# New per-engine orders, statistics by per-partition scalars and fewer warm-up matmuls in a retention and SoLU kernel

## Chip, cores and metric

The kernel runs on one core of a Trainium2 chip. The metric is device time in microseconds (us), the median over runs.

## What is computed

A retention step over q, k and v (8 batches, 8 heads, 576 positions, head size 64), whose output becomes 4,608 tokens of width 512, followed by a feed-forward block with a SoLU activation and a layer norm:

```python
scores = scale * np.matmul(q, k.transpose(0, 1, 3, 2))
gamma = 1.0 - 2.0 ** (-5.0 - np.arange(H, dtype=np.float32))
Dmat = np.where(rel >= 0, gamma[:, None, None] ** rel[None, :, :], 0.0)
attn_out = np.matmul(scores * Dmat[None, :, :, :], v)
x = np.ascontiguousarray(attn_out.transpose(0, 2, 1, 3)).reshape(B * S, H * D)
h = x @ w_in                                  # 512 -> 1024
h_max = np.max(h, axis=-1, keepdims=True)
e = np.exp(h - h_max)
solu = h * (e / (np.sum(e, axis=-1, keepdims=True) + 1e-09))
mu = np.mean(solu, axis=-1, keepdims=True)
var = np.mean((solu - mu) ** 2, axis=-1, keepdims=True)
out = ((solu - mu) / np.sqrt(var + 1e-06) * g_ln) @ w_out   # 1024 -> 512
```

Retention is computed in chunks: inside a chunk by scores and a mask, between chunks by a state k-transposed times v that is carried on with a decay.

## The kernel before

**Tiles.** The sequence of a batch is cut into two windows of 256 positions and a rest of 64; the rests of four batches form one window together. That makes 18 windows. A window is worked in two halves of four heads each, so there are 36 half-windows i. Each window also yields two blocks of 128 tokens, so there are 36 token tiles t for the feed-forward part.

**Steps of a half-window i.** `ldq`, `ldk`, `ldv` load 256 KB each (SP queue). `sq`, `sk` scale q and k to 16 bit and `cv` casts v (GpSimd, called POOL; for i = 0 and 1 sq is on VectorE, called DVE, and cv on ScalarE, called ACT). `T` transposes q and k on TensorE (PE), `qe` takes them out of PSUM (ACT). `S` computes scores, `mask` multiplies them by the mask (DVE). `K` computes k-transposed times v into PSUM. `sa` and `sd` add it to the carried state (DVE), `sm` multiplies by the decay (POOL, L441) and `sc` casts the state to 16 bit in two instructions (POOL, L450). `I` multiplies q by that state, `V` the masked scores by v, into the same PSUM tile, which `xe` takes out as xT (ACT). The last windows of a group of four batches (i = 16, 17, 34, 35) have no K and no state steps. K of the next half-window comes after V of this one, so K, sa, sd, sm, sc, I, V form a loop through three engines.

**Steps of a token tile t.** `M1` is the product with w_in, eight matmuls (L468). `em` negates it out of PSUM and finds the row minimum (DVE, L479), `ex` the exponential with its row sum se (ACT, L491), `so` the product of the two with its row sum su (DVE, L501; this is VectorE's product), `va` the row sum sv of the squared deviations (ACT, L510). `L` transposes the product and `le` takes it out (ACT). `M2` is the product with w_out (L560). For the first NE = 14 tiles the mean is removed after M2 by `od` (DVE); for later ones the weights are centred beforehand (`wp`, DVE). `x` (per window, L519 and L522, on DVE) makes the variance from se and sv, `rs` its power of -0.5 (POOL, L530), `oe` scales the output tile (ACT) and `out` stores it (SP).

**Order.** Every engine works its instructions strictly in program order. The table FIRST (L29 to L102) holds one written list of step names for each engine and for the SP queue. `order_ops` (L113) replays these lists with the durations in DUR and buffer limits in CAP, only to interleave the emission; it never changes the order in a list. So what each engine does next is what FIRST says, and a step that isn't ready holds all that stands behind it on its engine. A load in SP's list stands behind stores that may still wait for their `oe`.

**Start.** Twelve matmuls on zeros run first (L747). Then, up to time WARM = 31 of the replayed schedule and ahead of the first M2, the gaps that the replay sees on PE are filled with further matmuls on zeros (L755), 33 in all.

Of the kernel before, what the change touches and what calls it, by code (L numbers as in the profile page):

```python
# [11 lines left out]
P = 128  # L12
# [6 lines left out]
    sq=1.03, sk=1.03, st_b=0.4, cast=0.84, rs=0.6, cv=0.61,  # L19
    ld=0.89, ldw=1.34, out=0.72, lm=0.42,  # L20
# [4 lines left out]
WARM = 31.0  # L25
NE = 14
WPOOL = ()

FIRST = dict(  # L29
    ACT=(  # L30
        "cv1 cv0 qe0 xe0 qe1 qe2 wi1a wi3a wi2a xe1 wi0a ex0 xe2 qe3 qe4 ex1 le0 xe3 qe5 wg6 va1 "
        "le1 wg2 wg0 wg4 xe4 ex2 nw va0 qe6 xe5 ex3 le2 oe0 va2 ex4 qe7 oe1 va3 qe8 xe6 qe9 xe7 "
        "oe2 le3 va4 ex5 oe3 le4 va5 qe10 xe8 ex6 xe9 le5 oe4 qe12 ex7 ex8 le6 oe5 qe11 xe10 va6 "
        "va7 le7 xe11 ex9 oe6 qe13 va8 va9 oe7 le8 xe12 ex10 qe14 ex11 xe13 le9 va10 oe8 qe15 "
        "ex12 xe14 le10 oe9 va11 qe16 va12 xe15 le11 oe10 ex13 qe17 ex14 qe18 oe11 xe16 va13 le13 "
        "va14 le12 xe17 ex15 qe19 oe13 le14 va15 qe20 ex17 xe18 oe12 qe21 ex16 xe19 oe14 qe22 "
        "va17 le15 va16 ex18 oe15 le16 le17 xe20 oe16 xe21 ex19 va18 qe23 va19 oe17 ex20 le18 "
        "xe22 qe24 ex21 xe23 oe18 le19 va21 le20 va20 oe19 qe25 xe24 ex23 qe26 oe20 xe25 ex22 "
        "le21 va23 qe27 va22 le23 oe21 le22 ex24 qe28 xe26 ex25 xe27 oe22 qe29 va24 va25 ex26 "
        "le24 oe23 qe30 xe28 le25 oe24 qe31 ex27 xe29 oe25 va26 qe32 va27 le26 ex28 le27 xe30 "  # L40
        "ex29 xe31 oe26 qe33 va28 va29 oe27 ex30 le28 ex31 xe32 qe34 xe33 oe28 qe35 va31 le29 "
        "va30 xe34 ex32 le30 xe35 ex33 oe29 va32 va33 ex35 oe30 le31 va35 le32 ex34 oe31 le35 "
        "va34 le34 oe32 oe35 le33 oe34 oe33"
    ),
    DVE=(
        "sq1 sq0 sa0 sd0 mask0 sa1 sd1 mask1 wi1b wi2b sa2 gc sd2 wi3b wi0b mask2 em0 sa3 sd3 so0 "
        "em1 mask3 wg7 so1 sa4 sd4 mask4 em2 wg1 wg5 wg3 mask5 sa5 em3 sd5 so2 x0 wp3 wp0 sa6 od0 "
        "sd6 mask6 em4 so3 od1 em5 sa7 sd7 mask7 so4 x1 od2 sa8 mask8 sd8 em6 od3 so5 sa9 mask9 "
# [12 lines left out]
        "T0 K0 S0 I0 V0 T1 K1 S1 T2 I1 S2 V1 K2 G M1_0 I2 V2 T3 K3 M1_1 T4 S3 L0 I3 V3 S4 K4 T5 "
        "M1_2 L1 I4 V4 K5 S5 M1_3 WM M2_0 T6 I5 V5 K6 S6 L2 M1_4 M2_1 T7 M1_5 I6 T8 V6 K7 S7 M2_2 "
        "T9 I7 V7 S8 K8 L3 M1_6 M2_3 I8 V8 K9 S9 L4 M1_7 T10 M2_4 I9 V9 K10 S10 L5 M1_8 T12 M2_5 "
        "L6 M1_9 T11 I10 V10 K11 S11 M2_6 L7 I11 V11 K12 S12 T13 M1_10 M2_7 I12 L8 V12 S13 K13 "
        "M1_11 T14 M2_8 I13 V13 K14 S14 L9 M1_12 T15 M2_9 L10 I14 V14 S15 K15 M1_13 T16 M2_10 I15 "
        "V15 S16 L11 M1_14 T17 M2_11 T18 I16 S17 V16 M1_15 L13 I17 V17 K18 S18 L12 M2_13 T19 "
        "M1_17 L14 I18 S19 V18 K19 T20 M2_12 M1_16 T21 M2_14 I19 V19 S20 K20 T22 M1_18 L15 I20 "
        "V20 S21 K21 M2_15 L16 M1_19 L17 M2_16 I21 V21 K22 S22 T23 M1_20 M2_17 I22 S23 V22 K23 "
        "L18 M1_21 T24 M2_18 I23 V23 S24 K24 L19 M1_23 L20 M2_19 T25 I24 M1_22 V24 K25 S25 T26 "
        "M2_20 I25 V25 S26 K26 L21 M1_24 T27 M2_21 L23 I26 V26 K27 S27 L22 M1_25 T28 M2_22 I27 "  # L70
        "V27 K28 S28 T29 M1_26 M2_23 L24 M1_27 T30 I28 V28 S29 K29 L25 M2_24 T31 I29 V29 K30 S30 "
        "M2_25 M1_28 T32 I30 V30 S31 K31 L26 M1_29 L27 M2_26 I31 V31 K32 S32 T33 M1_30 M2_27 "
        "M1_31 L28 I32 V32 S33 K33 T34 M2_28 I33 V33 S34 T35 M1_32 L29 I34 S35 V34 L30 M1_33 I35 "
        "V35 M2_29 M1_35 L31 M2_30 M1_34 L32 M2_31 L35 M2_32 L34 M2_35 L33 M2_34 M2_33"
    ),
    POOL=(
        "sk0 sm0 sc0 sk1 sk2 sq2 sm1 sc1 cv2 sm2 sc2 sq3 sk3 cv3 sk4 sq4 sm3 sq5 sc3 cv4 sk5 cv5 "
        "sm4 sc4 sk6 sq6 cv6 sm5 sc5 sk7 sk8 rs0 sq8 sq7 sm6 cv8 sc6 cv7 sq9 sk9 sm7 sc7 cv9 rs1 "
        "cv11 sk10 sm8 sc8 sq12 sq10 cv13 cv10 sm9 sc9 sk12 rs2 sq11 sm10 sc10 sk11 cv12 sq13 "
        "sq16 sk13 sm11 sc11 sq14 sk14 rs3 sm12 sc12 cv14 sm13 sc13 sq15 cv16 sk15 sm14 rs4 cv17 "  # L80
        "sc14 sk16 cv15 cv18 sm15 sc15 sq17 rs5 sk17 sk18 sq18 sq19 sk19 sq21 cv19 rs6 sk21 sk20 "
        "sm18 cv21 sc18 sq20 sq22 sk22 sm19 sc19 cv20 rs7 sm20 sc20 cv22 sk23 rs8 sq23 cv25 sm21 "
        "sk24 sc21 sm22 sq24 cv23 sc22 cv24 sk25 sq25 sm23 rs9 cv26 sc23 sk26 sq26 sm24 sq27 sc24 "
        "rs10 sm25 sc25 sq29 sk27 sm26 cv28 cv29 sc26 cv27 sk28 cv30 sq28 sk29 rs11 sm27 sc27 "
        "sq30 sq31 sk30 sk31 sm28 sc28 rs12 sq32 cv32 sm29 sc29 sq34 sm30 sc30 sk32 cv35 cv31 "
        "sk33 sm31 sq33 sc31 rs13 cv33 sq35 sk34 sm32 sc32 sk35 cv34 sm33 sc33 rs14 rs15 rs16 "
# [3 lines left out]
        "ldk0 ldq1 ldv1 ldq0 ldv0 ldk1 lm ldv2 ldq2 ldk2 lwi3 lwi1 lwi2 lwi0 ldq3 ldk3 ldv3 ldk4 "  # L90
        "ldq4 ldq5 ldk5 ldv4 lwo6 ldv5 lwo0 lwo2 lwo4 ldk6 ldq6 ldv6 ldk7 ldv7 ldk8 ldq9 ldq8 "
        "ldq7 ldk9 ldv8 ldk10 ldq10 ldv9 out0 ldv11 ldv10 ldk12 ldq12 ldk11 ldv12 out1 ldv16 out2 "
        "ldv13 ldq16 ldq15 ldq13 ldk15 ldk14 out3 ldq11 ldk16 out4 ldk13 ldv17 ldv14 ldq14 ldk17 "
        "out6 ldq17 ldv15 ldq18 out5 ldq22 out7 ldv18 out8 ldk18 ldv21 ldv20 ldq19 ldk21 out9 "
        "ldk19 ldv19 ldk20 ldq21 ldq23 ldv22 ldv23 ldq20 ldk22 out11 out13 out10 ldk25 ldk24 "
        "ldv26 ldv25 ldq26 out12 ldk23 ldk29 ldv24 ldq25 ldv30 ldq24 ldk26 out14 out15 ldq27 "
        "out16 ldq31 ldk28 ldv27 ldv28 ldv29 out17 ldq28 ldv33 out18 ldk27 out19 ldq29 ldk31 "
        "ldq30 ldq32 ldv35 ldv31 ldk30 ldk33 out20 out22 ldq34 ldv32 ldk34 ldk32 out21 ldv34 "
        "ldq35 out23 ldk35 ldq33 out24 out26 out25 out27 out28 out29 out30 out31 out32 out35 "
        "out34 out33"  # L100
# [107 lines left out]
def kernel(  # L208
# [21 lines left out]
               xT=5, h=1, hn=3, e=2, oc=2, solu=3, sq=2, sml=8, lnT=4, o=1, osb=3)  # L230
# [52 lines left out]
    mhalf = small[:, 68:69]  # L283

# [156 lines left out]
    def state_cast(i):  # L443
        w, hf = divmod(i, 2)
        b, wi = wins[w]
        k = n_state[wi]
        n_state[wi] += 1
        s16 = sbd[wi][k % len(sbd[wi])]
        for e in range(2):
            nc.gpsimd.tensor_copy(out=s16[ee[e], :, :, ee[e]], in_=st[i]["g"][ee[e]])  # L450
        cur.setdefault((b, hf), {}).update({"g": st[i]["g"], wi: s16})
# [63 lines left out]
    def stats(w):  # L515
        d = ws[w]
        x = pools["sml"].tile([P, 2], FP, tag="w", name="w")
        d["x2"] = pools["sml"].tile([P, 2], FP, tag="w2", name="w2")
        nc.vector.scalar_tensor_tensor(  # L519
            out=x, in0=d["se"], scalar=1e-6, in1=d["se"], op0=ALU.mult, op1=ALU.mult  # L520
        )
        nc.vector.scalar_tensor_tensor(  # L522
            out=d["x2"], in0=d["sv"], scalar=float(DFF) ** -3, in1=x, op0=ALU.mult, op1=ALU.add
        )
# [263 lines left out]
```

## Time and profile before

| what | value |
|---|---|
| three runs | 246.45, 247.33, 356.75 us |
| median | 247.33 us |
| time of the profiled execution | 246.69 us |
| its span, first to last instruction | 244.9 us |
| busy: PE, DVE, ACT, POOL | 214.4, 182.9, 172.2, 172.7 us |
| mean granted TensorE clock | 0.992 |
| read from memory, written | 32.71 MB, 9.44 MB |

In the profile PE is the matmul engine and PEld its weight loads, which overlap it; a name with q at its end (SPq, POOLq) is an engine's sequencer. L468 is line 468 of the program. A row of the timeline gives start, length, engine, line, operation, output and input; in square brackets stands how long the engine sat idle before it and what released it. A window's row gives its length, then busy time (and instructions) of PE, PEld, DVE, ACT and POOL, the granted TensorE clock, the share of the DMA engines and GB/s; where only PE was asked for, its busy time alone stands ahead of the clock. Times lie on the span of one execution, 1.8 us shorter than that execution's device time.

### The profile page before, as it was taken

What the parts mean: (1) busy time and instruction counts of PE and PEld (TensorE: products, weight loads), DVE (VectorE), ACT (ScalarE), POOL (GpSimd) and SP (SyncE); (2) the same over time, 40 slices, a digit from 0 to 9 for tenths busy, and PEclk for the clock granted to TensorE, in tenths of its full rate; (3) what the DMA queues carried; (4) which work ended last, traced back from release to release, by engine and by line L of the source; (5) the groups of instructions that cost most, each with busy time, mean ns of one, the idle gap of its engine ahead of it and who ended that gap; (6) DMA issues with size and microseconds to landing.
All of it is one profiled execution on the core that took longest, in us unless ns stands there. A gap on an engine that the chain in (4) does not pass through costs nothing.

```text
span 244.9 us, 7426 instructions
## 1 busy us (share of the span) xinstructions
PE 214.4 (88%) x2998; PEld 124.1 (51%) x2998; DVE 182.9 (75%) x328; ACT 172.2 (70%) x301; POOL 172.7 (71%) x223
## 2 busy tenths in 40 slices
PE   8968887998997788999799889899869999999992
PEld 2435543554554445556456446455445554565550
DVE  7166899887995799989979767849845776897520
ACT  2234786767776597889769685868756687989971
POOL 2097994998959868799968969939995789631020
PEclk9999999999999999999999999999979999999999
DMA  7999999196886065798297865662516550510244
GB/s 188 322 367 300 352 295 269 30 246 170 226 236 185 3 170 175 193 305 237 63 256 196 264 175 136 170 172 82 178 29 188 156 150 4 129 46 23 65 94 120
DMA packets 65633, 42.62 MB, mean 174 GB/s; under 512 B 4024, under 2 KB 59456, under 8 KB 65600
## 3 DMA queue, kind: packets, MB, share of 16 engines
q1 hardware_dynamic: 65200, 41.96, 61.8%
q8 instruction: 23, 0.38, 0.6%
q10 hardware_dynamic: 400, 0.21, 0.4%
q14 instruction: 10, 0.08, 0.1%
HBM read 32.71 MB, written 9.44 MB: 172 GB/s over the span
## 4 chain that ended last, share of the span: by engine, by line
PE 33%; POOL 31%; DVE 13%; DMA 9%; issue 7%; ACT 5%; SPq 1%; POOLq 0%; DVEq 0%; ACTq 0%
POOL sbd L450 9%; PE h_ps L468 8%; POOL k L308 7%; PE o_ps L560 7%; POOL q L308 6%; PE xy L348 6%; POOL g L441 4%; DMA qr<-in_q_dram 4%; POOL v L316 3%; PE tln L536 3%; DVE ret L416 3%; DMA out_dram<-o_sb 2%; PE tqk L325 2%; DVE hn L479 2%; PE wm L755 2%
## 5 line engine op out<-in xcount | busy, mean ns | idle before, releaser
L468 PE MATMUL h_ps<-w_in,xT 128*128 128x512 f16 x288 | 68.8, 382 | 0.9 <-ACT w_in L612 0.9
L501 DVE SCALAR_TENSOR_TENSOR solu<-hn,e_sb 128x1024 f16<-128x1024 f32 x36 | 47.7, 1326 | 5.3 <-ACT e_sb L491 5.3
L479 DVE TENSOR_SCALAR_CACHE_REDUCE hn<-h_ps 128x1024 f32<-128x1024 f32 x36 | 43.8, 1218 | 9.9 <-PE h_ps L468 9.8
L491 ACT ACTIVATE e_sb<-hn,nm 128x1024 f32<-128x1024 f32 x36 | 41.4, 1151 | 8.0 <-DVE hn L479 6.2
L416 DVE TENSOR_TENSOR ret<-s_ps,masks 128x1024 f16<-128x1024 f32 x36 | 43.7, 1215 | 2.5 <-PE s_ps L383 2.5
L308 POOL TENSOR_TENSOR k<-kr,small 128x512 f16<-128x512 f32 x36 | 42.1, 1175 | 4.3 <-DMA kr<-in_k_dram 3.6
L510 ACT ACTIVATE sq<-solu,su 128x1024 f32<-128x1024 f16 x36 | 41.3, 1148 | 1.2 <-DVE solu L501 1.2
L308 POOL TENSOR_TENSOR q<-qr,small 128x512 f16<-128x512 f32 x34 | 39.4, 1165 | 3.7 <-DMA qr<-in_q_dram 3.0
L468 PEld LDWEIGHTS <-xT 128*128 128x128 f16 x288 | 27.0, 99 | 28.7 <-issue 2.0
L560 PEld LDWEIGHTS <-lnT 128*128 128x128 f16 x288 | 26.8, 98 | 28.7 <-issue 0.8
L441 POOL TENSOR_TENSOR g<-tt,small 128x128 f32<-128x128 f32 x32 | 17.1, 534 | 30.7 <-DVE tt L437 30.2
L560 PE MATMUL o_ps<-w2c,lnT 128*128 128x512 f16 x160 | 37.8, 379 | 0.1
L450 POOL CAST sbd<-g 64x256 f16<-64x256 f32 x64 | 34.8, 544 | 3.0
L456 ACT CAST xT<-xy 128x512 f16<-128x512 f32 x36 | 21.0, 584 | 21.3 <-PE xy L348 19.0
L333 ACT COPY qkT<-tqk 128x512 f32<-128x512 f32 x36 | 20.9, 579 | 15.4 <-PE tqk L325 15.3
L530 POOL TENSOR_TENSOR rs<-w,small 128x2 f32<-128x2 f32 x18 | 15.2, 846 | 20.3 <-DVE w L519 12.7
L348 PE MATMUL xy<-qkT,sbd 128*128 128x128 f16 (+1 forms) x128 | 13.5, 214 | 16.4 <-POOL sbd L450 15.8
L316 POOL CAST v<-vr 128x512 f16<-128x512 f32 x34 | 27.1, 801 | 0.8 <-PE xy L348 0.2
L560 PE MATMUL o_ps<-w2g,lnT 128*128 128x512 f16 x112 | 26.5, 379 | 0.6 <-DVE oc L568 0.6
L544 ACT COPY lnT<-tln 128x512 f32<-128x512 f32 x36 | 20.8, 577 | 5.7 <-PE tln L536 5.4
L536 PE MATMUL tln<-ident,solu 128*128 128x128 f16 x288 | 22.1, 220 | 0.5 <-ACT qkT L333 0.4
L536 PEld LDWEIGHTS <-solu 128*128 128x128 f16 x288 | 17.9, 98 | 6.5 <-issue 0.8
(53 smaller groups left out, 260.1 us busy)
## 6 DMA issues: line engine op xcount, KB each, us to landing
kr<-in_k_dram SPq DMA_DIRECT2D x32, 256.0 KB, 5.3
qr<-in_q_dram SPq DMA_DIRECT2D x32, 256.0 KB, 5.1
vr<-in_v_dram SPq DMA_DIRECT2D x32, 256.0 KB, 5.0
out_dram<-o_sb SPq DMA_DIRECT2D x64, 128.0 KB, 2.4
w_in_f<-in_moe_w_in_dram SPq DMA_DIRECT2D x4, 512.0 KB, 6.6
w_f<-in_moe_w_out_dram SPq DMA_DIRECT2D x4, 512.0 KB, 6.6
vr<-in_v_dram SPq DMA_DIRECT2D x16, 64.0 KB, 3.1
qr<-in_q_dram SPq DMA_DIRECT2D x16, 64.0 KB, 2.0
```

Source lines behind the costliest of these rows:

```text
L308: eng.tensor_tensor(out=t.rearrange("p j h d -> p h j d"), in0=st[i][nm + "r"], in1=g_of(i, base), op=ALU.mult,)
L316: copy(out=t, in_=st[i]["vr"])
L348: nc.tensor.matmul(start=(c, e) not in begun, stop=False, skip_group_check=True, **kw)
L416: nc.vector.tensor_tensor(out=d["ret"].rearrange("p e h j q -> p (e h) (j q)"), in0=d["s"].rearrange("p e h j q -> p (e h) (j q)"), in1=ma ...
L450: nc.gpsimd.tensor_copy(out=s16[ee[e], :, :, ee[e]], in_=st[i]["g"][ee[e]])
L468: nc.tensor.matmul(out=h_ps[:, hh], lhsT=st[2 * w + dc // 2]["xT"][:, c, dc % 2], rhs=w_in16[:, dc, hh], start=(dc == 0), stop=(dc == 3),)
L479: nc.vector.tensor_scalar(out=d["hn"], in0=d["h"], scalar1=-1.0, scalar2=None, op0=ALU.mult, op1=ALU.min, accum_out=d["nm"],)
L491: nc.scalar.activation(out=d["e"], in_=d["hn"], func=ACT.Exp, scale=-1.0, bias=d["nm"], accum_out=ws[w]["se"][:, c : c + 1],)
L501: nc.vector.scalar_tensor_tensor(out=d["solu"], in0=d["hn"], scalar=1.0, in1=d["e"], op0=ALU.mult, op1=ALU.mult, accum_out=ws[w]["su"][:, ...
L510: nc.scalar.activation(out=x, in_=tk[t]["solu"], func=ACT.Square, scale=-float(DFF), bias=ws[w]["su"][:, c : c + 1], accum_out=ws[w]["sv"] ...
L536: nc.tensor.transpose(out=tp[:, c], in_=d["solu"][:, c * P : (c + 1) * P], identity=ident)
L560: nc.tensor.matmul(out=d["o"], lhsT=d["lnT"][:, c], rhs=(w2g16 if t < NE else w2c16)[:, c], start=(c == 0), stop=(c == 7))
```

## The change

1. All five lists in FIRST are new. They hold the same steps, except that `x` is now one step per token tile (x0 to x35) instead of one per window (x0 to x17). The heads of the lists:

```diff
     ACT=(
-        "cv1 cv0 qe0 xe0 qe1 qe2 wi1a wi3a wi2a xe1 wi0a ex0 xe2 qe3 qe4 ex1 le0 xe3 qe5 wg6 va1 "
+        "cv0 qe0 cv1 wi2a qe1 qe2 wi0a xe0 wi1a xe1 wi3a qe3 ex0 xe2 wg2 qe4 xe3 ex1 va0 le0 wg4 "
...
     DVE=(
-        "sq1 sq0 sa0 sd0 mask0 sa1 sd1 mask1 wi1b wi2b sa2 gc sd2 wi3b wi0b mask2 em0 sa3 sd3 so0 "
+        "sq0 sa0 sd0 sq1 mask0 wi1b sa1 wi2b sd1 mask1 wi0b sa2 gc wi3b sd2 mask2 em0 sa3 sd3 "
...
     PE=(
-        "T0 K0 S0 I0 V0 T1 K1 S1 T2 I1 S2 V1 K2 G M1_0 I2 V2 T3 K3 M1_1 T4 S3 L0 I3 V3 S4 K4 T5 "
+        "K0 T0 G S0 T1 I0 V0 K1 T2 S1 I1 V1 K2 S2 M1_0 T3 I2 V2 K3 S3 M1_1 T4 I3 V3 S4 K4 M1_2 L0 "
...
     POOL=(
-        "sk0 sm0 sc0 sk1 sk2 sq2 sm1 sc1 cv2 sm2 sc2 sq3 sk3 cv3 sk4 sq4 sm3 sq5 sc3 cv4 sk5 cv5 "
+        "sk1 sk0 sq2 sk2 sm0 sc0 sm1 sc1 cv2 sk3 sm2 sq3 sc2 cv3 sk4 sq4 sm3 sc3 cv4 cv5 sk5 sq5 "
...
     SP=(
-        "ldk0 ldq1 ldv1 ldq0 ldv0 ldk1 lm ldv2 ldq2 ldk2 lwi3 lwi1 lwi2 lwi0 ldq3 ldk3 ldv3 ldk4 "
+        "ldv0 ldk1 ldq0 ldk0 ldq1 ldq2 lm lwi2 ldk2 ldv1 lwi1 lwi0 ldk3 ldv2 lwi3 ldq3 ldv3 ldq4 "
...
```

The ends of PE's and SP's lists:

```diff
-        "V35 M2_29 M1_35 L31 M2_30 M1_34 L32 M2_31 L35 M2_32 L34 M2_35 L33 M2_34 M2_33"
+        "L31 V35 M2_29 M1_34 M2_30 L33 M1_35 L32 M2_33 M2_32 L34 M2_31 L35 M2_34 M2_35"
...
-        "out34 out33"
+        "out34 out35"
```

2. The statistics: two instructions per token tile on one column each, with the other operands as per-partition scalars, in place of two per window on two columns.

```diff
-    def stats(w):
+    def stats(t):
+        w, c = divmod(t, 2)
         d = ws[w]
-        x = pools["sml"].tile([P, 2], FP, tag="w", name="w")
-        d["x2"] = pools["sml"].tile([P, 2], FP, tag="w2", name="w2")
-        nc.vector.scalar_tensor_tensor(
-            out=x, in0=d["se"], scalar=1e-6, in1=d["se"], op0=ALU.mult, op1=ALU.mult
-        )
-        nc.vector.scalar_tensor_tensor(
-            out=d["x2"], in0=d["sv"], scalar=float(DFF) ** -3, in1=x, op0=ALU.mult, op1=ALU.add
-        )
+        col = slice(c, c + 1)
+        x = pools["sml"].tile([P, 1], FP, tag="w", name="w")
+        if "x2" not in d:
+            d["x2"] = pools["sml"].tile([P, 2], FP, tag="w2", name="w2")
+        nc.vector.tensor_scalar(
+            out=x, in0=d["se"][:, col], scalar1=d["se"][:, col], scalar2=1e-6,
+            op0=ALU.mult, op1=ALU.mult,
+        )
+        nc.vector.tensor_scalar(
+            out=d["x2"][:, col], in0=d["sv"][:, col], scalar1=float(DFF) ** -3, scalar2=x,
+            op0=ALU.mult, op1=ALU.add,
+        )
...
+        op(f"x{t}", "DVE", "x", [f"va{t}"], (m + 2, 0.6), lambda t=t: stats(t), [("sml", [f"oe{t}"])])
         if c:
-            op(f"x{w}", "DVE", "x", [f"va{t - 1}", f"va{t}"], (m + 2, 0.6), lambda w=w: stats(w))
-            op(f"rs{w}", "POOL", "rs", [f"x{w}"], (m + 2, 0.77), lambda w=w: rstd(w), [("sml", [f"oe{t}"])])
+            op(f"rs{w}", "POOL", "rs", [f"x{t - 1}", f"x{t}"], (m + 2, 0.77), lambda w=w: rstd(w))
```

The pool `sml` of the small tiles gets 16 buffers instead of 8.

3. The fill on TensorE: a table in place of the gaps seen by the replay. The twelve matmuls at the start stay; 13 others take the place of 33.

```diff
-WARM = 31.0
+FILL = dict(K0=3, I0=6, I1=3, M1_0=1)
...
-        end_pe, fill = 0.0, True
         for o in sorted(ops, key=lambda o: start[o.name]):
             if o.eng == "PE":
-                fill = fill and o.name[:2] != "M2"
-                if fill and 6.0 < start[o.name] < WARM:
-                    for _ in range(int((start[o.name] - end_pe - 0.3) / 0.36)):
-                        nc.tensor.matmul(out=wm, lhsT=zeros[:, :P], rhs=zeros, start=True, stop=True)
-                end_pe = start[o.name] + o.dur
+                for _ in range(FILL.get(o.name, 0)):
+                    nc.tensor.matmul(out=wm, lhsT=zeros[:, :P], rhs=zeros, start=True, stop=True)
             o.emit()
```

4. Two switches that are off: XBAR (token tiles whose transpose would go through a DMA) and CASTD (state casts that would go to VectorE) are empty tuples, so no step takes their branch. The planner `order_ops` itself is as it was.

## The prediction

> **What bounds it now.** I read the chain of waits first (page, part 4), then the chain's opening, the table of waits, single rows of GpSimd and VectorE in the timeline, and windows of 20 and 2 us.
>
> ```profile
> PE 33%; POOL 31%; DVE 13%; DMA 9%; issue 7%; ACT 5%; SPq 1%; POOLq 0%; DVEq 0%; ACTq 0%
> ```
> No engine bounds it alone: TensorE and GpSimd take turns. The opening of the chain (start, length, what):
>
> ```profile
> 1.19 4.94 PE wm L748 x12
> 6.12 4.96 PE wm L755 x23
> 11.09 0.45 PE tqk L325 x8
> 12.53 0.40 POOL g L441
> ```
> The path runs through 23 warm-up matmuls. Scaled q and k of tile 0 were ready at 8.19 (its DVE row: 7.50 + 0.69) and 5.29 (POOL row: 4.25 + 1.04), yet the transposes T0 begin at 10.92, and GpSimd idles 7.24 us before 12.53. Waits (total, times, longest):
>
> ```profile
> POOL g L441 <- DVE tt L437: 30.2, 18, 7.2
> ...
> PE xy L348 <- POOL sbd L450: 15.8, 17, 2.6
> ```
> The second row is TensorE waiting for the state cast (`sc`) before I. The state loop K, sa, sd (DVE), sm, sc (POOL), I, V, next K is what TensorE's other matmuls must cover. What lengthens its GpSimd part:
>
> ```profile
> 40.44 1.21 DVE L501 SCALAR_TENSOR_TENSOR solu<-hn,e_sb 128x1024 f16<-128x1024 f32 x1
> 40.60 1.31 POOL L441 TENSOR_TENSOR g<-tt,small 128x128 f32<-128x128 f32 x1 [3.04 <-DVE tt L437]
> ```
> A multiply of 0.40 us takes 1.31, ending just after VectorE's product. Minimum/median/maximum ns of four rows:
>
> ```profile
> L308 POOL TENSOR_TENSOR k<-kr,small x36: 1036/1042/2108, 4.2 to 210.8; 128x512 f16<-128x512 f32 x36
> ...
> L450 POOL CAST sbd<-g x64: 386/398/1453, 13.0 to 214.4; 64x256 f16<-64x256 f32 x64
> ...
> L519 DVE SCALAR_TENSOR_TENSOR w<-se x18: 144/333/969, 41.6 to 234.0; 128x2 f32<-128x2 f32 x18
> ...
> L522 DVE SCALAR_TENSOR_TENSOR w<-sv,w x18: 160/163/973, 42.0 to 235.1; 128x2 f32<-128x2 f32 x18
> ```
> GpSimd's maxima are its minima plus about 1.05 us, one product. Count times (mean less minimum) is k 5.0, q 4.4, v 6.7, g 4.5, sbd 10.1, rs 2.9: 33.6 us, or 0.93 for each of 36 products. The two-element statistics also wait: 12.5 us against 18 x (0.144 + 0.160) = 5.5. Late in the run things change:
>
> ```profile
> 200.00:220.00 20.00, 19.44 (x295) 11.79 (x293) 16.24 (x31) 16.78 (x31) 13.20 (x18) 1.00 0.27 65
> ```
> TensorE (first figure) is 97% busy; this stretch and the tail can hardly shrink. TensorE's work after I33 is 24.6 us in the old order and 24.2 in the new (M1, M2 1.73, T, L 0.45 from the chain; I, S, V about 0.25).
>
> **The change, part by part.** The sum starts at the profiled execution's 246.69 us (span 244.9); the median is 0.64 higher.
>
> *Opening.* 23 + 10 warm-ups become 13, three of them before K0. The first five loads were taken up at 4.25, 5.18, 6.58, 7.50, 8.40, so a load lands about every 1.05 us. In the new SP order ldk0 is fourth, so sk0 runs 7.5 to 8.5, and K0 and T0 begin near 8.6: 2.3 us earlier than T0 did. GpSimd then does sk1, sk0, sq2, sk2 before sm0. ldq2, sixth, lands near 9.3. ldk2 follows masks and a quarter of w_in, 0.9 MB behind it, 3 us at the 299 to 306 GB/s of the rows 6 to 10 us: 12.4 at the latest, 10.3 by the page's GB/s per slice, cumulated to the 2.5 MB that end with ldk2. Thus sk2, sm0, sc0, sm1, sc1 end at 14.2 to 16.2, where sc1 ended at 18.36: 2.2 to 4.2 us earlier. M1_0 (21.47) needs all of w_in, whose last quarter now stands 0.26 MB (0.8 us) later in the queue; this can eat the gain. Fewer fills can also cost clock:
>
> ```profile
> 178.00:180.00 2.00, 0.55 (x18) 0.93 0.00 0
> 180.00:182.00 2.00, 2.00 (x53) 0.50 0.03 8
> 182.00:184.00 2.00, 2.00 (x8) 0.72 0.50 116
> ```
> After TensorE's 2.58 us wait the granted clock was 0.50: transposes 0.97 instead of 0.45, M1 2.39 instead of 1.73, with the small matmuls some 1.7 us lost. A 2.05 us wait (before 43.36) left it at 1.00. The new opening's gap is about 1.8 us (15 warm-ups end near 6.8), so no loss, at worst 1.7. The Trainium skill, "TensorE: Matmul & The Clock Gate", section "HAM oscillation", allows TensorE idle gaps up to about 3.4 us; the 2.58 us row is stricter. By the page alone the opening could lose nothing. Opening: gain 2.5, between -1.7 and 4.2.
>
> *Orders in the steady part.* Of the 15.8 us behind sc, 2.05 lie before 40 us (0.29, 0.58, 0.69, 0.49), leaving 13.8. Going through these waits, I compared the GpSimd steps between sd and sc with their minima: stretch in front of the waits that ended at 43.36, 56.14, 66.85, 81.77, 87.72, 121.24, 147.25, 179.45 is 1.41, 1.06, 0.46, 0.88, 0.91, 1.37, 1.03, 1.98 = 9.1 us, two thirds. An order that puts products elsewhere can save these; but 36 products of about 1 us must lie beside something, and a wait saved lets the next one show (k or q transposes, xT). I take two thirds of 9.1: 6. Bounds: 13.8 gained, or as much again lost, since nothing in the text of the orders fixes the time of a product against GpSimd. I add 1 for the clock loss behind the 2.58 us wait (0 to 1.7).
>
> *SP.* Each load behind a store waits for that tile's M2 and oe. TensorE work between that M2 and the load's reader: ldv13 10.6, ldk13 11.1, ldq11 12.8 at the smallest in the old order, 13.7 (ldq14) in the new. Before q of tile 11 GpSimd sat idle 2.98 us (68.56 to 71.54), I10 came 9.5 us after I9. Gain 1, between 0 and 3: part of that idle time lay beside TensorE work.
>
> *Statistics.* 36 instructions become 72, of [128,1]. Nearest rows without lock: 0.059 (memset 128x1, L741) to 0.160 (L522's minimum); I take 0.10, by the 0.08 of the 128x1 accumulator reads. The second waits for the first: 0.11 each (L519 ended 41.92, L522 began 42.03). So 72 x 0.10 + 36 x 0.11 = 11.2 against 12.5 + 18 x 0.11 = 14.5: 3.3 us less VectorE time, between 6.3 less and 1.0 more; if they wait as L519 does (0.333), 28.0, so 13.5 more. VectorE's 62 us of idle time hide it: nothing in the sum. Without that cover it is its share of the chain, 13% of 13.5, or 1.8 us. The added wait is on each `va`: behind x in VectorE's queue stand mask, em, so and sd, hence S, M1's buffer and the state loop. Old joins waited 1.4 us in all; the new ones mostly stand 4 to 20 places behind their product. The Trainium skill speaks against the edit: "VectorE: DVE Perf Modes", "The perf-mode tier table", gives tensor_scalar on fp32 in SBUF a mode using both read ports, and "SBUF — State Buffer", "SBUF: two separate sides", counts that mode among those that exclude GpSimd. By it the 13.5 us more, and a forecast 1.8 higher, would hold. No row shows a one-element tensor_scalar; 128x512 ones (L616) took 0.593 to 1.258.
>
> *End.* The last store becomes tile 35's, four 64 KB transfers on two queues (0.92 issue, 2.3 landing), where 4.1 us followed the last oe: 0.5, between 0 and 0.9.
>
> *Nothing:* `sml` 16 only uses memory; XBAR and CASTD are empty.
>
> Sum: 246.69 - 2.5 - 6 - 1 - 1 - 0.5 = 235.7 us.
>
> **Rivals.** *Opening only.* The new orders separate nothing on the chip and waits move. For: TensorE work between K and I, the loop's cover, averages 4.05 before and 4.19 after, with 11 tiles under 3 us in both. Against: GpSimd's minima (143 us) plus 36 x 0.93 = 176 us fit in the 210 from 4.2 to 214, so room is there. 246.7 - 2.5 = 244.2, chance 0.22.
>
> *Slower: joins on the squares.* x reaches VectorE before `va` has ended. If each of 36 waits 0.97, as the longest old one did (before 235.08), it decides where VectorE has no slack:
>
> ```profile
> 80.00:100.00 20.00, 16.64 (x262) 9.95 (x266) 18.05 (x31) 15.08 (x27) 16.18 (x22) 1.00 0.41 115
> 100.00:120.00 20.00, 19.38 (x300) 11.90 (x291) 19.20 (x32) 17.20 (x31) 17.68 (x21) 1.00 0.77 218
> 120.00:140.00 20.00, 18.20 (x258) 10.69 (x258) 17.90 (x32) 14.34 (x26) 16.57 (x19) 1.00 0.83 230
> ```
> VectorE (third figure) is busy 55.15 of 60 us: 11 tiles x 0.97 = 10.7 against 4.85 idle, +5.8; 20 to 80 us (busy 51.0 of 60, ten tiles: 9.7 against 9.0) adds 0.7. With the opening's gain and none from the products 250.7, without both 253. Against: the joins' places. Chance 0.15.
>
> *The whole gain:* all 13.8 with the opening's 4.2 gives 224; chance 0.03.
>
> **How the numbers follow.** The forecast, 235.7 with its own range 229 to 242, has 0.60. Two per cent, about what a measurement here can tell from no change, is 4.9 us: faster means below 242.4. Faster: 0.60 + 0.03 and a little of the opening-only case, 0.64. Slower: most of the joins case, 0.12. Same: 0.24. Range 229 to 246: it takes in opening-only; left out are the joins (0.15) and the low end (0.05).
>
> **What would show it.** K0 near 8.6 and sc1 before 16.2; granted clock 1.00 from 6 to 22 us; TensorE's wait for sbd at 8 to 10 us; stretch of sm and sc smaller though GpSimd's total stretch stays near 30; x rows near 0.10 and never 0.3 (else the lock holds); no 3 us idle of GpSimd for q; the tail unchanged. Wrong if sbd's wait stays near 15, if x waits for sq by more than 5 us, or if a new wait on xT, k or hn takes its place.

## The result and the profile after

The changed kernel takes 228.26 us (median of four, 226.25 to 230.43) against 247.82 us for the kernel before: a ratio of 0.920, 95% interval 0.911 to 0.930. The median is 7.4 us below the forecast of 235.7 and 0.7 us below the low end of the range. The ratio leaves out the slow executions (230.43 us, and 356.75 us of the kernel before). The profiled execution took 228.07 us, its span is 226.0 us; 18.9 us of span are gone (244.9 before).

The chain of waits of the changed kernel, shares by engine:

```profile
PE 51%; POOL 20%; ACT 7%; DVE 7%; DMA 6%; issue 5%; SPq 2%; POOLq 0%; DVEq 0%; ACTq 0%
```

TensorE holds half of the path instead of a third. GpSimd fell from 31% to 20%, VectorE from 13% to 7%. TensorE's busy time went from 214.4 to 209.4 us, so of the 18.9 us that the span lost 5.0 are work (mostly the 20 warm-up matmuls that fell away) and 13.9 are idle time.

The table of waits of the changed kernel (total, times, longest):

```profile
...
POOL g L444 <- DVE tt L440: 12.1, 12, 2.5
...
POOL k L311 <- DMA kr<-in_k_dram: 7.0, 3, 3.8
...
PE xy L351 <- POOL sbd L453: 3.5, 7, 0.9
...
POOL q L311 <- DMA qr<-in_q_dram: 2.2, 2, 1.5
...
DVE w L532 <- ACT sq L515: 1.4, 2, 1.2
```

The third row is the wait that the prediction watched: TensorE waits for the state cast 3.5 us instead of 15.8. The 7.0 us that GpSimd waits for k lie in the opening (3.75, 1.72 and 1.53 us, before 5.01, 7.78 and 12.14). The last row is what the slower rival needed: the new joins wait 1.4 us for the squares, no more than the old ones.

The same rows of GpSimd and VectorE as before, with minimum/median/maximum ns (L311 was L308, L444 was L441, L453 was L450, L528 and L532 are the new statistics):

```profile
L311 POOL TENSOR_TENSOR k<-kr,small x36: 1037/1042/2027, 5.0 to 192.2; 128x512 f16<-128x512 f32 x36
L311 POOL TENSOR_TENSOR q<-qr,small x34: 1037/1043/2022, 9.6 to 188.4; 128x512 f16<-128x512 f32 x34
```

```profile
L444 POOL TENSOR_TENSOR g<-tt,small x32: 395/400/1376, 13.1 to 195.1; 128x128 f32<-128x128 f32 x32
```

```profile
L453 POOL CAST sbd<-g x64: 388/401/1302, 13.6 to 196.0; 64x256 f16<-64x256 f32 x64
```

```profile
L528 DVE TENSOR_SCALAR w<-se x36: 198/204/213, 36.5 to 216.8; 128x1 f32<-128x1 f32 x36
```

```profile
L532 DVE TENSOR_SCALAR w<-sv,w x36: 213/214/218, 36.8 to 218.2; 128x1 f32<-128x1 f32 x36
```

GpSimd's maxima are still one product above the minima, but their counts moved. Count times (mean less minimum) gives 5.9 us for k, 6.8 for q, 8.6 for v, 2.3 for g, 2.6 for sbd and about 3.1 for rs: some 29 us in all, against 33.6 before. The state steps g and sbd fell from 14.6 to 4.9 us and the conversions q, k, v rose from 16.1 to 21.3. So the products still hold up GpSimd for nearly as long as before; they now collide more with conversions, which TensorE needs later, and less with the state loop. One such collision in the timeline of GpSimd (start, length):

```profile
64.08 0.84 POOL L444 TENSOR_TENSOR g<-tt,small 128x128 f32<-128x128 f32 x1
64.88 2.02 POOL L311 TENSOR_TENSOR k<-kr,small 128x512 f16<-128x512 f32 x1
66.85 0.85 POOL L453 CAST sbd<-g 64x256 f16<-64x256 f32 x2
```

VectorE's product ran from 64.57 to 65.99; the conversion of k took 2.02 us instead of 1.04, and the casts behind it their own 0.85. The two statistics vary by 15 and 5 ns over 36 instructions each: in this kernel they never wait for GpSimd, and cost 0.20 and 0.21 us.

Windows of 20 us of the changed kernel (length, then busy time of PE, PEld, DVE, ACT, POOL, granted clock, DMA share, GB/s):

```profile
40.00:60.00 20.00, 19.46 (x292) 11.76 (x291) 18.64 (x38) 16.36 (x29) 19.35 (x24) 1.00 0.90 237
60.00:80.00 20.00, 19.41 (x272) 11.22 (x270) 19.23 (x38) 16.70 (x30) 17.88 (x24) 1.00 0.64 175
80.00:100.00 20.00, 19.05 (x306) 11.73 (x305) 19.61 (x40) 16.27 (x30) 16.63 (x22) 1.00 0.67 184
```

TensorE is busy 57.9 and VectorE 57.5 of these 60 us. Before, the same windows gave TensorE 51.2 and VectorE 51.0. Two engines are now full at the same time; this turns out to be the point that the prediction missed.

The time came from the middle. Starts of the row minima em, token tile by token tile, show it: the sixth em began at 50.8 before and 50.7 now, the eleventh at 86.4 and 77.2, the twenty-first at 146.0 and 133.4, the last at 229.7 and 212.2. So there is no gain in the first 50 us, 9 us by the eleventh token tile, 13 by the twenty-first, 17.5 at the last em, and 1.4 more behind it.

### The profile page after: what moved, and what is told of

Its sections match the earlier page's. It is cut to its first block, busy times and chain, and to the rows that moved or that the text cites. A ratio compares the mean times of both kernels' runs of the same rounds, so it can differ in the third digit from the quotient of the medians.

```text
span 226.0 us, 7417 instructions
## 1 busy us (share of the span) xinstructions
PE 209.4 (93%) x2978; PEld 122.5 (54%) x2978; DVE 182.1 (81%) x364; ACT 171.6 (76%) x301; POOL 168.5 (75%) x223
## 4 chain that ended last, share of the span: by engine, by line
PE 51%; POOL 20%; ACT 7%; DVE 7%; DMA 6%; issue 5%; SPq 2%; POOLq 0%; DVEq 0%; ACTq 0%
PE h_ps L473 15%; PE o_ps L576 15%; PE xy L351 7%; POOL k L311 6%; POOL sbd L453 5%; PE tqk L328 5%; PE tln L547 4%; POOL q L311 3%; DMA qr<-in_q_dram 3%; ACT xT L461 3%; DMA kr<-in_k_dram 2%; POOL g L444 2%; POOL v L319 2%; PE s_ps L386 2%; SPq L296 2%
## 5 line engine op out<-in xcount | busy, mean ns | idle before, releaser
L311 POOL TENSOR_TENSOR k<-kr,small 128x512 f16<-128x512 f32 x36 | 43.1, 1200 | 7.8 <-DMA kr<-in_k_dram 7.0
L311 POOL TENSOR_TENSOR q<-qr,small 128x512 f16<-128x512 f32 x34 | 41.9, 1237 | 6.3 <-PE h_ps L473 3.6
L473 PEld LDWEIGHTS <-xT 128*128 128x128 f16 x288 | 26.4, 98 | 27.1 <-ACT xT L461 1.4
L453 POOL CAST sbd<-g 64x256 f16<-64x256 f32 x64 | 27.5, 429 | 3.0
L319 POOL CAST v<-vr 128x512 f16<-128x512 f32 x34 | 28.8, 856 | 0.6
L444 POOL TENSOR_TENSOR g<-tt,small 128x128 f32<-128x128 f32 x32 | 14.9, 466 | 12.5 <-DVE tt L440 12.1
```

The costliest lines, as they stand in the source:

```text
L311: eng.tensor_tensor(out=t.rearrange("p j h d -> p h j d"), in0=st[i][nm + "r"], in1=g_of(i, base), op=ALU.mult,)
L319: copy(out=t, in_=st[i]["vr"])
L453: (nc.vector if i in CASTD else nc.gpsimd).tensor_copy(out=s16[ee[e], :, :, ee[e]], in_=st[i]["g"][ee[e]])
L473: nc.tensor.matmul(out=h_ps[:, hh], lhsT=st[2 * w + dc // 2]["xT"][:, c, dc % 2], rhs=w_in16[:, dc, hh], start=(dc == 0), stop=(dc == 3),)
```

## The experiments

Three mechanisms could carry the gain, and the theories were about their sizes: the collision of VectorE's product with GpSimd (called the exclusion below), loads that stand behind stores in SP's list, and the statistics. The five lists of an order wait on each other and were written together; lists of the one order weren't mixed with lists of the other engine by engine. Ratios are to the kernel before on the same chip in the same batch. The median of the kernel before lay between 246.2 and 248.8 us in these batches, so a difference between ratios of two batches is known to about one point, and the medians stand beside it where the two disagree.

### Statistics alone, and all but the statistics

The first kernel takes the second part of the change alone (statistics per token tile, two entries x in VectorE's list where one stood, 16 buffers). The second is the changed kernel with the old statistics (x per window at the place of its second x):

```diff
...
-        nc.vector.tensor_scalar(
-            out=x, in0=d["se"][:, col], scalar1=d["se"][:, col], scalar2=1e-6,
-            op0=ALU.mult, op1=ALU.mult,
-        )
...
+        nc.vector.scalar_tensor_tensor(
+            out=x, in0=d["se"], scalar=1e-6, in1=d["se"], op0=ALU.mult, op1=ALU.mult
+        )
...
```

> The kernel before with the statistics of the change alone: 72 tensor_scalar on one column, each pair where the old list had its one step. Theory A (the gain comes from the lists, which take VectorE's product out of the state loop's GpSimd steps): no effect beyond 1%, 245 to 250 us, TensorE's wait for the state cast still 13 to 17 us; the statistics rows constant at 0.20 and 0.21 us. Theory C (the statistics' waits on GpSimd held up VectorE, and the form removed that): 238 to 243 us.

> The changed kernel with the old statistics: 18 pairs of scalar_tensor_tensor on two columns, where the later of each two new steps stood. Theory A: 226 to 231 us, no more than 1% from the changed kernel; the statistics rows again at a median near 0.3 us with maxima near 0.9, because they wait for GpSimd. Theory C: 234 us or more.

Measured: 1.0055 [1.0012, 1.0098] (248.51 us) for the statistics alone, 0.942 [0.937, 0.947] (232.63 us) for the rest alone. In the old order the new statistics are worth nothing, by a hair less. In the new order the old form costs 2.2 points of ratio, 5.4 us (4.4 by the medians). Its statistics rows take no more time in sum than the new ones, 18 x (0.336 + 0.374) = 12.8 against 36 x (0.204 + 0.214) = 15.0 us; but VectorE is busy 3.4 us longer in all (185.5 against 182.1), since the product takes 3.1 us more (mean 1.427 against 1.341 us, 36 times). Whether the two-tensor form or the later place of the paired step costs the time, this run can't tell; a run further below keeps the places. So the two parts don't add: 1.4 us lost alone, 4.4 to 5.4 gained together.

### The exclusion taken away

Here the product leaves out the exponentials: it reads one tensor and a per-partition scalar (their row sum) instead of two tensors, in the old and in the new order:

```diff
-        nc.vector.scalar_tensor_tensor(
-            out=d["solu"], in0=d["hn"], scalar=1.0, in1=d["e"], op0=ALU.mult, op1=ALU.mult,
+        nc.vector.tensor_scalar(
+            out=d["solu"], in0=d["hn"], scalar1=ws[w]["se"][:, c : c + 1], scalar2=None, op0=ALU.mult, op1=ALU.add,
...
```

> The kernel before, in which VectorE's product leaves out the factor e: it multiplies hn by the row sum of the exponentials as a per-partition scalar, so it reads one tensor from SBUF and still waits for the same exponential. If its row stays near 1.2 us, only its second source is gone. Theory A: GpSimd's stretch (mean less minimum, 33.6 us) falls below 8, TensorE's wait for the state cast from 15.8 to 5 to 8, time 233 to 240 us. Theory B (the new lists are better for other reasons: loads, covers): stretch falls, but the time stays at 243 us or more. If the one-source form also excludes GpSimd, the stretch stays and the run says nothing on A or B.

> The changed kernel with the same product without the factor e. Theory A: the new lists already keep the product off the path, so little is left to gain: 223 to 228 us, at most 4 us less than the changed kernel. Theory B: as much gained as in the old lists.

Measured: 0.953 [0.946, 0.960] (234.86 us) in the old order, 0.9155 [0.908, 0.923] (225.96 us) in the new one, beside 0.920 for the change itself. Product and conversions of the old order without the second tensor:

```profile
L501 DVE TENSOR_SCALAR_CACHE_REDUCE solu<-hn,se x36: 1264/1273/1280, 25.6 to 220.5; 128x1024 f16<-128x1024 f32 x36
```

```profile
L308 POOL TENSOR_TENSOR k<-kr,small x36: 1035/1042/1044, 3.8 to 198.7; 128x512 f16<-128x512 f32 x36
```

The product keeps its length, and the conversions lose their second value: the longest of 36 took 1.044 us instead of 2.108. TensorE's wait for the cast fell from 15.8 to 7.9 us. So taking the exclusion away gains 4.7% of the old order, 11.7 us, and 0.5%, 1.1 us, of the new one (2.3 by the medians), where the two intervals overlap. The new orders save some 10 us here, hardly by less collision (29 us against 33.6) but by cheaper places for it. How much of the small gain in the new order is the places, and how much that other engines end at the same time there, these two runs don't separate.

### Loads ahead of stores

In the old order three loads were moved ahead of stores that they stood behind: q 11 ahead of those of tiles 1 to 3, v 13 of that of tile 2, k 13 of those of tiles 3 and 4; then the same with the one-source product; then with the new statistics too:

```diff
-        "... ldk12 ldq12 ldk11 ldv12 out1 ldv16 out2 "
-        "ldv13 ldq16 ldq15 ldq13 ldk15 ldk14 out3 ldq11 ldk16 out4 ldk13 ldv17 ..."
+        "... ldk12 ldq12 ldk11 ldq11 ldv12 out1 ldv13 "
+        "ldv16 out2 ldq16 ldq15 ldq13 ldk15 ldk14 ldk13 out3 ldk16 out4 ldv17 ..."
```

> The kernel before, with three loads moved ahead of the stores they stood behind in SP's list: q of 11, k of 13, v of 13. Theory L (a load held behind a store costs several us that are not won back): GpSimd's 3 us wait for q goes, the tenth minimum em comes 4 to 6 us earlier (before: 86.4), time 240 to 244 us. Theory A alone (only the exclusion matters, the held loads lie beside other work): 246 us or more.

> The same three loads earlier, and the product with one source, as in the old lists' run before. If the two causes add up: 234.9 less 4 to 6, so 228 to 231 us, within 2 to 5 us of the new lists with the same product (226.0). If the loads matter only behind the exclusion: 233 us or more.

> The old lists with the three loads earlier, the product with one source and the new statistics. If VectorE's statistics matter as soon as the other two causes are out of the way: 228 to 230 us, 2 to 4 less than without the new statistics (232.2). If the old lists keep VectorE's slack, so that its own time doesn't count: 231 to 234 us.

Measured: 0.990 [0.985, 0.995] (246.1 us), 0.936 [0.931, 0.942] (232.21 us) and 0.946 [0.939, 0.952] (232.0 us). GpSimd around the load of q 11 with the three loads moved:

```profile
67.65 0.69 POOL L529 TENSOR_TENSOR rs<-w,small 128x2 f32<-128x2 f32 x1
68.30 1.04 POOL L307 TENSOR_TENSOR q<-qr,small 128x512 f16<-128x512 f32 x1
```

There is no idle time in brackets any more where the kernel before had 2.98 us (68.56 to 71.54), and the eleventh em (the expectation counts from zero) came at 84.4 instead of 86.4. Alone the loads are worth 1.0%, 2.5 us. Once the exclusion is gone they are worth 1.6 points, 4 us, by the ratios (0.936 against 0.953) and 2.7 us by the medians, so not clearly more. The new statistics on top gain nothing: 232.0 against 232.2 us by the medians, and a point lost by the ratios (0.946 against 0.936). In the old order they are worth nothing even without exclusion and held loads.

### The opening: more and fewer warm-up matmuls

The changed kernel with twelve warm-up matmuls ahead of K0 instead of three, and the kernel before with its fill cut to the change's number (`FILL = dict(T0=3, I0=6, I1=3, M1_0=1)`, T0 being its first step):

```diff
-FILL = dict(K0=3, I0=6, I1=3, M1_0=1)
+FILL = dict(K0=12, I0=6, I1=3, M1_0=1)
```

> The changed kernel with 12 warm-up matmuls before K0 instead of 3, which fill TensorE's 2.3 us gap before K0. Granted clock 1.00 up to 20 us instead of 0.86 and 0.78. If the opening is held by transfers (both kernels moved 12.1 MB in their first 40 us), the time stays within 1 us of 228; if the slow clock cost the opening's gain, 225 to 226.5 us.

> The kernel before in which only the fill is changed: 3, 6, 3 and 1 warm-up matmuls before T0, I0, I1 and M1_0 in place of the 33. T0 begins near 8.5 instead of 10.9. Prediction's view (the fill holds the path): 1.5 to 2.5 us less than before, first minimum em near 21.5 instead of 23.4. Theory D (the first 40 us are held by transfers, 12.1 MB in both kernels): within 1 us of before, the em at 50 us unmoved.

Measured: 228.47 us, 0.912 [0.903, 0.921], and 245.32 us, 0.994 [0.989, 0.999]. The opening of the changed kernel, two windows, and the same with twelve:

```profile
6.00:12.00 6.00, 3.26 (x49) 2.23 (x48) 2.81 (x5) 0.59 (x1) 2.14 (x3) 0.73 1.13 338
12.00:22.00 10.00, 8.54 (x131) 4.45 (x129) 5.73 (x12) 4.84 (x9) 6.00 (x11) 0.82 1.11 341
```

```profile
6.00:12.00 6.00, 5.24 (x66) 2.87 (x64) 3.36 (x5) 0.58 (x1) 2.24 (x4) 1.00 1.10 336
12.00:22.00 10.00, 7.07 (x131) 3.59 (x130) 5.64 (x13) 4.83 (x9) 6.73 (x13) 1.00 1.11 341
```

In this profile the clock went back to 1.00 and the sixth em began at 49.7 instead of 50.7, but the median stayed. The twelve fills don't settle what the clock costs: of the four executions two had a mean granted clock of 1.000 and 0.999 and took 225.68 and 226.71 us, the two others 0.992 and 0.982 and took 230.23 and 230.53. The changed kernel itself took 226.25 us at a mean of 1.000, and 228.07 and 228.45 at 0.980 and 0.991. So an execution that keeps the clock may be 1 to 2 us faster; no run sets the clock alone.

The DMA share reads above 1 in all four rows: the loads run without a pause. Over the first 40 us both the kernel before and the changed one moved 303 GB/s x 40 us = 12.1 MB, and in the profiles of all twenty kernels the sixth em begins between 49.0 and 51.8. That fits an opening that is set by transfers, which neither order nor clock moves by more than 1 to 2 us; no run changed the transfers to show it. In the old order fewer fills save 1.4 us.

### VectorE's time in both orders

Four kernels change VectorE's work by a known amount. The first gives the changed kernel the old two-tensor instruction for each of its 72 statistics:

```diff
-        nc.vector.tensor_scalar(
-            out=x, in0=d["se"][:, col], scalar1=d["se"][:, col], scalar2=1e-6,
-            op0=ALU.mult, op1=ALU.mult,
-        )
...
+        nc.vector.scalar_tensor_tensor(
+            out=x, in0=d["se"][:, col], scalar=1e-6, in1=d["se"][:, col], op0=ALU.mult, op1=ALU.mult
...
```

The second and third add a third statistic, unused, to every tile of the new order and of the old order with the new statistics (`nc.vector.tensor_scalar(out=y, ...)` with the operands of the first). The fourth needs only one per tile in the new order: the product carries the factor (1024^3 x 1e-6)^-0.5, the output weights a factor that makes up for it, and x2 = se x se + sv is a single instruction with two per-partition scalars.

> The changed kernel in which only the form of the statistics is the old one: scalar_tensor_tensor on one column, 72 of them, in the places of the new ones. If the form (two tensors, which wait for GpSimd) cost the 4.4 us that the new lists lost with the old statistics: 231 to 235 us, rows with a median near 0.3 and maxima near 1 us. If it was the later place of the paired step: 227 to 230 us.

> The changed kernel with a third, unused statistics instruction per tile: 7.4 us more for VectorE, in the same places, without any wait on GpSimd. If VectorE's own time counts in the new lists: 230 to 234 us. If only waits on GpSimd did (the two-tensor form), within 1 us of 228.

> The old lists and the old fill with the new statistics and a third, unused instruction of the same kind on every token tile (36 more, about 7.4 us of VectorE work). In the new lists the same addition cost 2.2%. If the old lists have slack on VectorE where the new ones have none, the time stays within 1% of the old lists with two statistics (248.5 us): 246 to 250. If added VectorE work costs in any order, it rises by 4 us or more, to 252 and above.

> The changed kernel with one statistics instruction per tile instead of two: the constant between the two terms is moved into the product's scalar and into the scale of the output weights, so the same result is computed. VectorE has 36 x 0.2 = 7.4 us less to do. If VectorE's time is on the path of the new lists between 40 and 100 us (busy 18.6 to 19.6 of 20): 224 to 227 us. If it isn't: within 1 us of 228.

Measured: 0.950 [0.943, 0.957] (235.46 us), 0.942 [0.937, 0.947] (232.25 us), 1.012 [1.008, 1.016] (249.79 us) and 0.927 [0.920, 0.935] (229.02 us). The two-tensor statistics in the new order, and its windows:

```profile
L528 DVE SCALAR_TENSOR_TENSOR w<-se x36: 143/165/1016, 35.4 to 223.9; 128x1 f32<-128x1 f32 x36
```

```profile
60.00:80.00 20.00, 17.80 (x257) 10.30 (x256) 19.87 (x34) 14.27 (x25) 15.95 (x22) 1.00 0.64 174
80.00:100.00 20.00, 17.07 (x238) 10.00 (x240) 19.54 (x36) 15.12 (x27) 16.15 (x21) 1.00 0.50 139
```

Their minimum, 0.143, is below the 0.198 of the new form, but they wait for GpSimd up to a whole instruction (mean 0.321 and 0.297): the one that began at 82.23 ended at 83.20, just after GpSimd's conversion of k from 82.14 to 83.18. That is 36 x (0.321 + 0.297) = 22.2 us against 15.0, 7.2 us more, and the kernel takes 7.2 us more too: 235.46 less 228.26. As the places are the same, the form alone does it. In the windows VectorE (third figure) is at 39.4 of 40 us, and TensorE has fallen from 38.5 to 34.9.

The third statistic adds 36 x 0.204 = 7.3 us. In the new order it costs 2.2 points, 5.4 us (4.0 by the medians); in the old order 0.7 points beyond the two statistics, 1.6 us (1.3 by the medians). So added VectorE time counts at about 0.5 to 1 in the new order and at 0.2 in the old. The single statistic takes time away, though less than its expectation reckoned, because its row is longer:

```profile
L527 DVE TENSOR_SCALAR w<-se,sv x36: 256/265/274, 35.7 to 219.7; 128x1 f32<-128x1 f32 x36
```

The rows take 36 x 0.266 = 9.6 us instead of 15.0, and yet it gained nothing. Added work costs, removed work doesn't pay.

### What stands behind VectorE in the new order

Why doesn't it pay? In the run with one statistic the twelfth em began 1.5 us earlier than in the changed kernel (79.9 against 81.4) and the thirteenth 1.5 us later (90.4 against 88.9). A late load seemed to eat the gain. First I suspected the loads of half-window 18, which stand behind two or three stores; the second run also has the single statistic and twelve warm-up matmuls:

```diff
-        "... ldk15 out7 out6 ldk19 ldk18 ldk21 ldv20 out8 ldq22 ldv18 "
-        "ldv23 ldq18 ldk22 out10 ..."
+        "... ldk15 ldk18 ldv18 ldq18 out7 out6 ldk19 ldk21 ldv20 out8 ldq22 "
+        "ldv23 ldk22 out10 ..."
```

> The changed kernel with the loads of k, v and q of half-window 18 moved ahead of the stores of tiles 7 and 6 in SP's list, behind which the load of k was held until 86.67 us. If this held load is what limits the new lists next, the gap of 7.5 us between em of tiles 11 and 12 closes by 2 to 4 us and the end follows: 224 to 226.5 us. If something else holds there (the state steps on GpSimd or VectorE's list), the time stays within 1 us of 228.3.

> The changed kernel with the three loads moved as in the run beside this one, one statistic per token tile in place of two (the constant goes into the product's scalar and the weights' scale, same result) and twelve warm-up matmuls ahead of K0 in place of three. If a held load is what hid the removal of 7.4 us of VectorE work, this run is 2 to 4 us faster than the one beside it: 220 to 224 us. If VectorE's work counts only when it is added, it equals the run beside it within 1 us.

Measured: 0.917 [0.912, 0.922] (227.37 us) and 0.918 [0.909, 0.927] (229.08 us): no difference from the change, so the suspicion fell. The trace of the run with one statistic names another load. GpSimd there:

```profile
78.27 1.04 POOL L311 TENSOR_TENSOR q<-qr,small 128x512 f16<-128x512 f32 x1 [3.24 <-DMA qr<-in_q_dram]
79.28 0.40 POOL L444 TENSOR_TENSOR g<-tt,small 128x128 f32<-128x128 f32 x1
```

This is q of half-window 14; the state step of half-window 12 stands behind it in GpSimd's list. In the changed kernel the same wait is 1.50 us. Its load stands behind v 16, v 15 and the store of tile 5, so three more runs put it ahead of them, alone, with one statistic, and with the three other loads:

```diff
-        "... ldk17 ldq16 ldv16 ldv15 out5 ldq14 ldq20 out4 ..."
+        "... ldk17 ldq16 ldq14 ldv16 ldv15 out5 ldq20 out4 ..."
```

> The changed kernel with one entry of SP's list moved: the load of q for half-window 14 stands ahead of the loads of v 16 and v 15 and the store of tile 5. In the profiles of the new lists GpSimd sits idle 1.5 to 3.4 us for it near 77 us, ahead of the state steps of half-window 12, and the profiled executions with 3.2 and 3.4 us of that wait are those of 229 us. If this load is what limits there, the wait goes, the gap between em of tiles 11 and 12 is 7 us or less and the time is 225 to 227 us. If not, the time stays at 227.4 to 228.3 us.

> The same move with one statistic per token tile in place of two (the constant goes into the product's scalar and the weights' scale, same result). If the late load of q is what hid the removal of 7.4 us of VectorE work (em of tile 11 was 1.5 us earlier, em of tile 12 was 1.5 us later), this run is 1.5 to 3 us faster than the one beside it. If VectorE's work counts only when it is added, it equals the run beside it within 1 us.

> The move of the load of q for half-window 14 together with the loads of k, v and q of half-window 18 ahead of the stores of tiles 7 and 6. If both groups of loads hold, it is 1 to 2 us faster than the move of q 14 alone; if the loads of half-window 18 hold nothing, it equals it within 1 us.

Measured: 0.923 [0.918, 0.928] (227.63 us), 0.922 [0.917, 0.928] (227.4 us) and 0.923 [0.918, 0.928] (227.59 us). GpSimd's wait for that load is gone, and the thirteenth em still begins at 88.9. The chain of waits of the first of the three, over this place (start, length, what):

```profile
75.89 1.23 DVE solu L506 x2
77.12 0.20 DVE tt L440
77.32 1.14 DVE hn L484 x2
78.46 1.14 DVE ret L419
...
79.83 0.21 DVE w L532
80.04 0.66 DVE oc L584
...
80.85 0.21 DVE w L532
...
81.23 0.21 DVE w L532
81.44 1.14 DVE hn L484 x2
82.58 0.21 DVE g L433
...
82.89 0.30 DVE tt L440
...
83.26 0.40 POOL g L444
...
84.16 0.41 POOL sbd L453
```

With the load on time, the path runs through an unbroken row of VectorE's instructions from 75.89 to 83.19, three pairs of statistics among them, to the state step of half-window 13. The changed kernel has the same VectorE instructions at the same times to within 0.02 us. So load and VectorE end there together. But moving both isn't enough either: in the second of the three runs the same state step still begins at 83.40, and the chain reaches it through ScalarE:

```profile
77.66 2.37 ACT sq L515 x4
80.03 0.47 ACT lnT L555
80.50 1.14 ACT e_sb L496 x2
81.64 0.47 ACT lnT L555
82.11 0.50 ACT xT L461
...
82.63 0.30 DVE g L433
...
83.03 0.30 DVE tt L440
...
83.40 0.40 POOL g L444
```

Three paths end at this place within 0.2 us, and TensorE has little idle time behind them: in that run it is busy 38.7 of the 40 us from 60 to 100, as against 38.5 in the changed kernel, and what remains idle of TensorE between 40 and 200 us in the changed kernel is 4.9 us in all, spread over the eight windows. So there is hardly anything left to gain from VectorE alone. None of these versions beats the change by more than its interval.

## Why the forecast was too high, step by step

Two measured blocks stand against the sum. All but the statistics was forecast at 11.0 us (2.5 + 6 + 1 + 1 + 0.5) and measured at 14.3 (5.8% of 247.1). The statistics were forecast at nothing and measured at 5.4 on top (4.4 by the medians).

**The failed step is the one that set the statistics at nothing.** It said: "VectorE's 62 us of idle time hide it". That idle time is of the old order. It is true there: the same edit is worth -1.4 us, and a third statistic costs 1.6 us. But the edit comes with lists that pull 6.7 us of TensorE idle time out of 40 to 100 us, and with it VectorE's: 57.5 of 60 us are busy, and there a third statistic costs 4.0 to 5.4 us, the two-tensor form at the same places 7.2 us, and the old statistics as they were, one paired step per window, 4.4 to 5.4 us. How that last figure divides between the form and the later place of the step stays open. The working needed one more line: in the order that is forecast, what is VectorE's share? The prediction's own slower rival asked that, priced added joins against 4.85 us of idle time in three windows, and used it only against the change.

**Products against GpSimd: right mechanism, mis-sized.** Forecast 6, bounds 13.8 gained or as much lost. The exclusion is worth 11.7 us in the old order and 1.1 in the new, so some 10 were saved, and TensorE's wait for the cast fell to 3.5 us where 8 to 10 were forecast. Two thirds of the visible stretch before the waits was too careful: "a wait saved lets the next one show" did not happen to that extent. That GpSimd's total stretch would stay near 30 us while its state steps' share shrinks came out as stated: 29 us, and 4.9 of them in g and sbd (14.6 before).

**Held loads: sized too small.** Forecast 1; in the old order the three loads are worth 2.5 us alone and 2.7 to 4 behind the removed exclusion. How much of that the new list keeps isn't measured; after the opening GpSimd waits there 1.50 us for q 14 and 3.55 us ahead of q 18 (before 101.66), and both waits go when these loads are moved, but moving them, alone or together, gains nothing clear.

**Opening: forecast 2.5, next to nothing by the sixth em (50.8 before, 50.7 now).** K0 began at 8.87, near the 8.6 of the prediction, but sc1 ended at 18.24 and not before 16.2. The chain's opening shows why:

```profile
8.87 0.43 PE xy L351 x12
9.30 0.98 PE tqk L328 x8
...
11.59 0.97 PE tqk L328 x8
12.56 2.56 PE wm L771 x6
15.12 0.83 PE xy L351 x31
```

The prediction summed GpSimd's steps and left out TensorE between them: the six fills ahead of I0 took 2.56 us, 0.43 each instead of the 0.22 of the 23 fills before, at the fallen clock. That clock was the second miss: 1.00 was forecast from 6 to 22 us, and it was 0.73 from 6 to 12 and 0.82 from 12 to 22. TensorE had waited 2.27 us for k 0 (6.60 to 8.87), longer than the 1.8 us reckoned. Nor does the length of one wait decide, as the prediction took it to: with the single statistic a wait of 2.39 us before K0 left the clock at 1.00, with the new statistics in the old order one of 2.53 us (before 178.41) did too, and in the old order with fewer fills one of 2.05 us (before 43.02) was followed by 0.51. The Trainium skill, "TensorE: Matmul & The Clock Gate", section "HAM oscillation", puts the gap that costs the clock at about 3.4 us; in the traces here 2.05, 2.27 and 2.58 us were enough in some executions. In the profile with twelve warm-ups the sixth em came 1.0 us earlier, and in that with four loads moved, which has the same opening, 1.7 us, both at a clock of 1.00 up to there. So the fallen clock may have cost 1 to 2 us; a run that sets the clock alone is missing.

**End: forecast 0.5.** After the last scaling of an output tile (221.60 + 0.69 = 222.29) 3.7 us remained, against 4.1: 0.4.

**The statistics' price: lock ruled out, row mis-sized.** "x rows near 0.10 and never 0.3" was half right: 0.198 to 0.218, never 0.3. The 0.10 had been taken from rows of other kinds (a memset, an accumulator read). So the new rows take 15.0 us and not 7.2, more than the 12.8 of the old form in the same order, and not less VectorE time as reckoned. The Trainium skill, "VectorE: DVE Perf Modes", section "The perf-mode tier table", together with "SBUF — State Buffer", section "SBUF: two separate sides", spoke for a lock; for one element per partition the 72 rows show none. What does take part is the instruction with two tensors, down to one element: 0.143 to 1.016 us.

**The rivals.** Opening only (244.2) fell with the 3.5 us wait for the cast. The slower rival, joins on the squares, fell with 1.4 us of such waits in all. The whole gain (224, chance 0.03) was nearer to the truth than the forecast, 4.3 us off against 7.4, but by luck: it took the opening's and the products' upper ends, and what came was much of the products and, in place of the opening, the statistics. The range's low end, 229, came from the forecast's own terms and had no room for a step set at nothing.

## What to carry to other kernels

When a change packs the engines more tightly, price its other edits in the packed order, not in the idle time of the old one: the same statistics were worth -1.4 us before and 4 to 5 us after. Where VectorE stood at 96%, added work cost half to all of its length and removed work gained nothing, since at the place looked at a load and ScalarE ended at the same time; so test an edit in both directions before its worth is put down to it. Collisions that can't be avoided can still be moved: the changed order has nearly as much of them (29 against 33.6 us), and taking them away gains 1 to 2 us there instead of 11.7.

## What was not expected of the hardware

- A one-column `tensor_scalar` on VectorE took 0.198 to 0.218 us in all 72 rows and never waited for GpSimd, 0.256 to 0.274 with two per-partition scalars; the two-tensor instruction on the same column took 0.143 at best and up to 1.025 us.
- A product of 1024 elements with one tensor and a per-partition scalar and a row sum took as long as one with two (1.27 us against 1.21 and more), and the conversions of k beside it kept to 1.035 to 1.044 us. It isn't shown for every `tensor_scalar`: four without a row sum on 512 columns (L632 of the changed kernel) varied from 0.494 to 0.800 us.
- The granted clock fell to half after waits of TensorE of 2.05, 2.27 and 2.58 us, and not after others of 2.05, 2.39 and 2.53 us, so the length of one wait alone doesn't decide.
